# Per-channel vectors of two-byte elements stored and loaded as rows, and convolution pools that wait tile by tile

## The chip, the cores and the metric

The kernel runs on one core of one Trainium2 chip. The metric is the device time of one execution in microseconds; lower is better. The kernel before takes 2185.29 us (median of 6 runs, 2183.25 to 2195.69).

## The reference

The forward function is `x + S4(LN(x)) + ReGLU(LN(x))` on a sequence of L = 2048 positions and D = 576 channels, with bfloat16 inputs. The kernel computes its output and the gradients of everything that has a weight, 13 outputs in all.

```python
xn = _layernorm(x)
# A: diagonal state space, N = 128 states for each channel
dt = jnp.exp(log_dt)[:, None]
P  = jnp.exp((dt * A)[:, :, None] * l[None, None, :])
K  = jnp.einsum("dn,dnl,dn->dl", Cc, P, dt * Bc).real
y  = irfft(rfft(K padded) * rfft(u padded))[:L] + u * Dskip
# B: gated FFN, F = 4608
h  = relu(xn @ W_gate) * (xn @ W_up);   out = h @ W_down
```

Two of the outputs are vectors of one number for each channel, 576 bfloat16 elements: the gradient of `Dskip` (`out_9`) and that of `log_dt` (`out_8`). One input has that shape and is read as such a vector: `log_dt`. Six more parameter gradients (`A_re`, `A_im`, `B_re`, `B_im`, `C_re`, `C_im`) have 576 x 128 elements.

## The kernel before

Channels lie on the partitions in five chunks: four of 128 and one of 64 (`dchunks`, NK = 5). Two streams of work are written into one program.

**The FFN** (`Ffn`, L162 to 427) is the main stream. The hidden width is cut into 12 chunks of 384, the sequence into 4 groups of 4 tiles of 128. For each chunk and group there are units: `a_unit` (L226) does the gate, up and down-gradient matmuls (L234), ACT makes `rg` and `upb` (L239, L241), DVE `upm`, `hT`, `dgT`, `duT`; `t_unit` (L255) transposes those on TensorE (L260); `outdx` (L263) multiplies them with the weights (L278), copies the result to `osx` (ACT or DVE, L65 or L59) and accumulates it in DRAM by a DMA of the POOL queue (L283); `osx` has 4 buffers. `dw_down`, `dw_gu` and `dw_left` (L298, L312, L329) make the weight gradients.

**The convolution** (`S4`, L441 to 942) is a Python generator. It has three phases: make the DFT tables, turn the parameters into the vectors needed (`params`, L518) and transform the two signals (phase 1); the kernel and the sums for its gradients, in blocks (L799, L820; phase 2); the parameter gradients, and then the outputs (phase 3). The main loop (L1050 to 1071) draws the next piece of it as soon as its estimated time is below 0.95 of the FFN's, and so mixes the two. A scheduler then orders the instructions for each engine; each engine runs its own list in order. Most loads and stores are issued from the SP queue, also in order, and go round eight DMA semaphores.

The places that the change touches:

- `dskip_out` (L151): after the fourth group of the layernorm, DVE sums the four partial skip gradients (`dsk_tot`, L154), casts them, and POOL stores five columns, each of 128 or 64 two-byte elements, one per partition (L158).
- `load_raw` (L509): for one chunk of channels, SP loads six matrices of 128 x 128 into `raw` (L511), then the `log_dt` column as `ldt` (L513), and ACT takes its exponential (L515) into `dt`. It is called five times in `params` and five times in phase 3.
- `param_grads` (L828): for one chunk, SP loads `R`; PE transposes it (L837), ACT copies it to `Gd`; then six times ACT scales a matrix by `dt` into `g_ob` (L850; pool of 2 buffers) and SP stores it (L851). At the end DVE has summed the `log_dt` gradient into `tot` and `dldb` (L873), and SP stores that column (L874).
- Behind the loop over the chunks, phase 3 loads `S3` (L902), `dsk`, and for each of 16 steps `bC` and two spectra (L910, L914), which PE turns (L583, L584).
- The pools of `S4` (L457) and of the final stage (L1047) are opened and closed stage by stage, and their memory is used again by the next.

Of the kernel before, what the change touches and what calls it, by code (L numbers as in the profile page):

```python
# [20 lines left out]
L, D, F, N = 2048, 576, 4608, 128  # L21
ST = 16
DH = D // 2
NK = 5
# [45 lines left out]
def dchunks():  # L70
    return [(k, k * P, min(P, D - k * P)) for k in range(NK)]
# [6 lines left out]
def make_consts(g):  # L78
    nc, consts = g.nc, g.consts
    g.ident_bf = consts.tile([P, P], BF16, name="ident_bf")  # L80
    make_identity(nc, g.ident_bf[:])
    g.ident_f = consts.tile([P, P], F32, name="ident_f")
    make_identity(nc, g.ident_f[:])
    g.hpcol = consts.tile([P, 1], F32, name="hpcol")
    nc.vector.memset(g.hpcol[:], math.pi / 2)
    g.rinv = consts.tile([P, ST], F32, name="rinv")
    g.dsk_acc = consts.tile([P, NK, NSG], F32, name="dsk_acc")
# [63 lines left out]
def dskip_out(g, small):  # L151
    nc = g.nc
    tot = small.tile([P, NK], F32, name="dsk_tot")
    nc.vector.tensor_reduce(out=tot[:], in_=g.dsk_acc[:], op=ALU.add, axis=AX.X)  # L154
    totb = small.tile([P, NK], BF16, name="dsk_totb")
    nc.vector.tensor_copy(totb[:], tot[:])
    for k, d0, dsz in dchunks():
        nc.gpsimd.dma_start(g.out_dskip[d0:d0 + dsz].rearrange("(p o) -> p o", o=1), totb[:dsz, k:k + 1])  # L158

# [281 lines left out]
class S4:  # L441
# [65 lines left out]
    def load_raw(self, pool, k, d0, dsz):  # L507
        nc = self.g.nc
        raw = pool.tile([P, 6, N], BF16, name="raw")  # L509
        for i, nm in enumerate(("A_re", "A_im", "B_re", "B_im", "C_re", "C_im")):  # L510
            nc.sync.dma_start(raw[:dsz, i, :], self.aps[nm][d0:d0 + dsz, :])  # L511
        ldt = pool.tile([P, 1], BF16, name="ldt")
        nc.sync.dma_start(ldt[:dsz], self.aps["log_dt"][d0:d0 + dsz].rearrange("(p o) -> p o", o=1))  # L513
        dt = pool.tile([P, 2], F32, name="dt")
        nc.scalar.activation(dt[:dsz, 0:1], ldt[:dsz], ACT.Exp)  # L515
        return raw, dt

    def params(self):  # L518
        g, nc, bal = self.g, self.g.nc, self.g.bal
        v = nc.vector  # L520
        with ExitStack() as c:
            rawp = self.pool(c, "par_raw", 2)
            parp = self.pool(c, "par_w", 2)
            todo = []

            def turn():
                pw, d0, dsz = todo.pop(0)
                Tt = parp.tile([P, 4, P], F32, name="Tt")
                ps = self.ps()
                for i in range(4):  # L530
                    nc.tensor.transpose(out=ps[:, i * P:i * P + dsz], in_=pw[:dsz, i, :], identity=g.ident_f[:dsz, :dsz])
                bal.copy(Tt[:, :, 0:dsz], ps[:].rearrange("p (i d) -> p i d", d=P)[:, :, 0:dsz], 4 * dsz)
                nc.sync.dma_start(self.T_dram[:, :, d0:d0 + dsz], Tt[:, :, 0:dsz])

            for k, d0, dsz in dchunks():
                raw, dt = self.load_raw(rawp, k, d0, dsz)
                Ar, Ai, Br, Bi, Cr, Ci = (raw[:dsz, i, :] for i in range(6))
                v.tensor_scalar(dt[:dsz, 1:2], dt[:dsz, 0:1], 1.0 / TWO_PI, None, op0=ALU.mult)
# [3 lines left out]
                v.tensor_scalar(pw[:dsz, 0, :], Ar, dt[:dsz, 0:1], None, op0=ALU.mult)  # L542
                v.tensor_scalar(pw[:dsz, 1, :], Ai, dt[:dsz, 1:2], None, op0=ALU.mult)
                v.tensor_tensor(p1[:dsz], Cr, Br, op=ALU.mult)
                v.tensor_tensor(p2[:dsz], Ci, Bi, op=ALU.mult)
                v.tensor_tensor(p1[:dsz], p1[:dsz], p2[:dsz], op=ALU.subtract)
                v.tensor_scalar(pw[:dsz, 2, :], p1[:dsz], dt[:dsz, 0:1], None, op0=ALU.mult)
# [3 lines left out]
                v.tensor_scalar(pw[:dsz, 3, :], p1[:dsz], dt[:dsz, 0:1], None, op0=ALU.mult)  # L551
# [276 lines left out]
    def param_grads(self, d0, dsz, raw, dt, pool, gp):  # L828
# [6 lines left out]
        ps = self.ps()  # L835
# [7 lines left out]
        dtk = dt[:dsz, 0:1]  # L843
# [30 lines left out]
        nc.sync.dma_start(self.outs["log_dt"][d0:d0 + dsz].rearrange("(p o) -> p o", o=1), dldb[:dsz])  # L874
        bal.add(d=4.5, a=1.5)
        yield 4.5

# [1 line left out]
    def phase3(self):  # L879
        g, nc, bal = self.g, self.g.nc, self.g.bal  # L880
        v = nc.vector
        with ExitStack() as c:
# [11 lines left out]
            with ExitStack() as c1:  # L894
                rawp = self.pool(c1, "p3_raw", 2)
                pool = self.pool(c1, "p3_g", 2)
                for k, d0, dsz in dchunks():
                    raw, dt = self.load_raw(rawp, k, d0, dsz)
# [3 lines left out]
            nc.sync.dma_start(self.S3[:], self.s3_dram[:])  # L902
# [21 lines left out]
            for n2 in range(ST):  # L924
# [4 lines left out]
                o = op.tile([P, 2, D], F32, name="base")  # L929
# [45 lines left out]
def kernel(  # L975
# [30 lines left out]
    nc = tc.nc  # L1006
    rows = lambda ap: ap.flatten_outer_dims().rearrange("(p t) d -> p t d", p=P)
    g = G()
# [35 lines left out]

    def final(t):
        if not fin:
            fin.extend(fctx.enter_context(tc.tile_pool(name=n, bufs=3)) for n in ("fin", "fin_small"))  # L1047
        final_tile(g, s4, fin[0], fin[1], t)

    sgen = s4.gen()  # L1050
# [53 lines left out]
```

## Time and profile before

| | |
|---|---|
| median of 6 runs | 2185.29 us |
| profiled execution | 2184.37 us |
| its span, first to last instruction | 2182.7 us |
| mean TensorE clock granted | 0.950 |
| TensorE (PE) busy | 1877.9 us, 86% |
| VectorE (DVE) busy | 1480.8 us, 68% |
| ScalarE (ACT) busy | 1522.0 us, 70% |
| GpSimd (POOL) busy | 259.6 us, 12% |
| moved from and to HBM | 364.29 MB, mean 167 GB/s |

The slices of the profile cut the span into 40 pieces of 54.6 us and give the busy share of each in tenths. A view of instructions in time gives start and duration in us, the engine, the line of the program, the operation and its operands; the bracket behind a row is how long the engine was idle ahead of it and what ended that. The list of waits gives the total, the number and the longest of the waits of one line for one releaser. "SPq" is the queue of the SyncE engine; "landing" is the time from the issue of a DMA until it is reported complete. Buffer numbers and some digits of names are left out of the profile (`out_dram` is any output, `S_26015` the tile `S3`).

### The profile page before, as it was taken

What the parts mean: (1) busy time and instruction counts of PE and PEld (TensorE: products, weight loads), DVE (VectorE), ACT (ScalarE), POOL (GpSimd) and SP (SyncE); (2) the same over time, 40 slices, a digit from 0 to 9 for tenths busy, and PEclk for the clock granted to TensorE, in tenths of its full rate; (3) what the DMA queues carried; (4) which work ended last, traced back from release to release, by engine and by line L of the source; (5) the groups of instructions that cost most, each with busy time, mean ns of one, the idle gap of its engine ahead of it and who ended that gap; (6) DMA issues with size and microseconds to landing.
All of it is one profiled execution on the core that took longest, in us unless ns stands there. A gap on an engine that the chain in (4) does not pass through costs nothing. (4 is left out here: it accounts for less than half of the span.)

```text
span 2182.7 us, 45801 instructions
## 1 busy us (share of the span) xinstructions
PE 1877.9 (86%) x17720; PEld 1280.2 (59%) x17720; DVE 1480.8 (68%) x3461; ACT 1522.0 (70%) x3304; POOL 259.6 (12%) x318
## 2 busy tenths in 40 slices
PE   6969999965899999899999999998735998889877
PEld 3645667543566766766766766666523665557545
DVE  7434655379989888798898888884323775642563
ACT  4745766477989989889989889896423763352562
POOL 5210110020101101101111111101000010010010
PEclk9989999986999999999999999999977999899989
DMA  9567799651545744635645545548418896895687
GB/s 285 187 147 241 221 274 286 213 130 14 113 119 116 156 118 98 144 103 100 146 101 114 154 109 114 124 104 223 145 47 134 252 276 220 270 316 138 169 248 206
DMA packets 259322, 364.29 MB, mean 167 GB/s; under 512 B 95840, under 2 KB 168672, under 8 KB 258336
## 3 DMA queue, kind: packets, MB, share of 16 engines
q1 hardware_dynamic: 228288, 297.65, 43.7%
q0 software_dynamic: 28704, 61.36, 18.4%
q8 instruction: 138, 2.26, 0.4%
q10 hardware_dynamic: 2112, 2.36, 0.3%
q14 instruction: 80, 0.66, 0.1%
HBM read 214.45 MB, written 146.84 MB: 166 GB/s over the span
## 5 line engine op out<-in xcount | busy, mean ns | idle before, releaser
L65 ACT CAST osx<-ps_mm 128x288 bf16<-128x288 f32 x708 | 280.8, 458 | 63.3 <-PE ps_mm L278 60.6
L283 POOL DMA_DIRECT2D acc_dram<-osx x176 | 152.0, 865 | 1345.6 <-ACT osx L65 1032.1
L278 PE MATMUL ps_mm<-wgT,dgT 128*128 128x288 bf16 x1152 | 215.1, 290 | 25.7 <-ACT osx L65 18.0
L312 PEld LDWEIGHTS <-xs 128*128 128x128 bf16 x1536 | 148.9, 98 | 113.3 <-DMA xs<-xs_dram_88 17.8
L278 PE MATMUL ps_mm<-wuT,duT 128*128 128x288 bf16 x1152 | 215.2, 290 | 0.0
L234 PE MATMUL ps_mm<-gT,wdT 128*128 128x512 bf16 x720 | 190.7, 385 | 7.8 <-DVE upm L243 4.9
L298 PE MATMUL ps_mm<-gq,hN 128*128 128x144 bf16 x2304 | 170.3, 230 | 23.7 <-DMA gq<-gq_dram_93 22.2
L298 PEld LDWEIGHTS <-hN 128*128 128x128 bf16 x2304 | 155.9, 100 | 32.1 <-issue 13.2
L243 DVE SCALAR_TENSOR_TENSOR upm<-ps_mm,upb 128x512 bf16<-128x512 f32 x144 | 99.0, 687 | 105.4 <-ACT upb L241 104.7
L312 PE MATMUL ps_mm<-dgN,xs 128*128 128x384 bf16 x768 | 146.1, 332 | 18.6 <-DMA xs<-xs_dram_88 17.3
L278 PEld LDWEIGHTS <-hT 128*128 128x128 bf16 x1152 | 108.1, 99 | 53.4 <-issue 18.5
L312 PE MATMUL ps_mm<-duN,xs 128*128 128x384 bf16 x768 | 139.2, 326 | 0.0
L278 PEld LDWEIGHTS <-dgT 128*128 128x128 bf16 x1152 | 113.1, 99 | 42.4 <-issue 14.0
L278 PEld LDWEIGHTS <-duT 128*128 128x128 bf16 x1152 | 113.6, 99 | 30.9 <-issue 1.0
L751 ACT ACTIVATE ysn<-yr 128x512 bf16<-128x512 f32 x144 | 98.2, 682 | 40.7 <-DVE yr L748 40.5
L234 PEld LDWEIGHTS <-wdT 128*128 128x128 bf16 x720 | 70.5, 99 | 84.7 <-issue 15.1
L65 ACT CAST obw<-ps_mm 128x384 bf16<-128x384 f32 x102 | 48.9, 479 | 99.8 <-PE ps_mm L312 83.2
L234 PE MATMUL ps_mm<-xT,wg_100 128*128 128x512 bf16 x360 | 102.2, 383 | 16.7 <-ACT upb L241 16.7
L65 ACT CAST dhb<-ps_mm 128x512 bf16<-128x512 f32 x144 | 89.3, 620 | 33.8 <-PE ps_mm L234 32.1
L753 ACT ACTIVATE ycs<-ya,hpcol 128x512 bf16<-128x512 f32 x144 | 112.3, 780 | 0.6
L278 PE MATMUL ps_mm<-wd_104,hT 128*128 128x288 bf16 x576 | 97.9, 292 | 13.9 <-ACT upb L241 9.8
L825 DVE TENSOR_REDUCE Sm<-pr 128x8 f32<-128x256 f32 x288 | 109.0, 410 | 0.1
(3111 smaller groups left out, 4647.2 us busy)
## 6 DMA issues: line engine op xcount, KB each, us to landing
acc_dram<-osx POOLq DMA_DIRECT2D x192, 288.0 KB, 4.5
gT<-gT_dram SPq DMA_DIRECT2D x44, 640.0 KB, 6.2
xT<-xT_dram SPq DMA_DIRECT2D x44, 640.0 KB, 5.2
out_dram<-obw SPq DMA_DIRECT2D x96, 96.0 KB, 2.5
base_dram<-base SPq DMA_DIRECT2D x16, 576.0 KB, 4.3
f_base<-base_dram SPq DMA_DIRECT2D x16, 576.0 KB, 5.6
gq<-gq_dram_91 SPq DMA_DIRECT2D x12, 576.0 KB, 3.6
gq<-gq_dram_92 SPq DMA_DIRECT2D x12, 576.0 KB, 4.3
```

Of the source, the lines that this page charges most:

```text
L65: self.nc.scalar.copy(out, in_)
L234: nc.tensor.matmul(ps[:], lhsT=w[:, k, fs], rhs=rhs[:, k, :], start=(k == 0), stop=(k == NK - 1))
L243: nc.vector.scalar_tensor_tensor(upm[:], ps_g[:], 0.0, upb[:], op0=ALU.is_gt, op1=ALU.mult)
L278: nc.tensor.matmul(ps[:, :DH], lhsT=lt[:, js], rhs=rh, start=(i == 0), stop=(i == len(mms) - 1))
L283: nc.gpsimd.dma_start(g.acc_dram[:, t, :, :], o[:], accum_op=ALU.add)
L298: nc.tensor.matmul(ps[:, (ft - f) * 144:(ft - f + 1) * 144], lhsT=self.hN[:, st, ft * P:(ft + 1) * P], rhs=gq[:, st, :], start=(st == 0), ...
L312: nc.tensor.matmul(ps[:, :Fc], lhsT=xs[:, st, :], rhs=src[:, st, :], start=(st == 0), stop=(st == ST - 1))
L751: nc.scalar.activation(sn[:], yr[:], ACT.Sin, scale=-TWO_PI)
L753: nc.scalar.activation(cs[:], ya[:], ACT.Sin, scale=-TWO_PI, bias=g.hpcol[:])
L825: nc.vector.tensor_reduce(out=Sm[:, vi, s0 + dd:s0 + dd + DG, :], in_=pr[:], op=ALU.add, axis=AX.X)
```

## The change

Three things are changed in the transfers of the vectors, and one in the pools.

1. A new function `col_store` takes the five columns as a [128, 5] tile, transposes it on TensorE into PSUM, lets DVE cast it into a row tile of 5 x 128 bfloat16, and stores it by two POOL DMAs: four rows of 128 elements, and the 64 left. `dskip_out` calls it once. `param_grads` leaves its result in a column of `g.dld`, and phase 3 calls `col_store` once behind the loop over the chunks.
2. A new function `load_dt` loads `log_dt` as five rows by two SP DMAs, takes one exponential, and turns it by one TensorE transpose into columns that stay in `g.dt`, beside a copy divided by 2 pi. `load_raw` no longer loads or computes it.
3. The pools of `S4` and of the final stage get `reuse_waits="tile"`: a tile in memory that was used before waits for the users of the earlier tiles on its own bytes, not for all users of the pools that were closed.

```diff
+def col_store(g, pool, psum, col, dst):
+    nc = g.nc
+    ps = psum()
+    nc.tensor.transpose(out=ps[:NK, :P], in_=col, identity=g.ident_f[:])
+    row = pool.tile([NK, P], BF16, name="row")
+    nc.vector.tensor_copy(row[:], ps[:NK, :P])
+    nf = NK - 1
+    nc.gpsimd.dma_start(dst[0:nf * P].rearrange("(k p) -> k p", p=P), row[0:nf, :])
+    nc.gpsimd.dma_start(dst[nf * P:D].rearrange("(o p) -> o p", o=1), row[nf:NK, 0:D - nf * P])
...
     nc.vector.tensor_reduce(out=tot[:], in_=g.dsk_acc[:], op=ALU.add, axis=AX.X)
-    totb = small.tile([P, NK], BF16, name="dsk_totb")
-    nc.vector.tensor_copy(totb[:], tot[:])
-    for k, d0, dsz in dchunks():
-        nc.gpsimd.dma_start(g.out_dskip[d0:d0 + dsz].rearrange("(p o) -> p o", o=1), totb[:dsz, k:k + 1])
+    col_store(g, small, lambda: g.psum_mm.tile([P, 512], F32, name="ps_mm"), tot[:], g.out_dskip)
...
-        return ctx.enter_context(self.g.tc.tile_pool(name=name, bufs=bufs))
+        return ctx.enter_context(self.g.tc.tile_pool(name=name, bufs=bufs, reuse_waits="tile"))
...
-        ldt = pool.tile([P, 1], BF16, name="ldt")
-        nc.sync.dma_start(ldt[:dsz], self.aps["log_dt"][d0:d0 + dsz].rearrange("(p o) -> p o", o=1))
-        dt = pool.tile([P, 2], F32, name="dt")
-        nc.scalar.activation(dt[:dsz, 0:1], ldt[:dsz], ACT.Exp)
-        return raw, dt
+        return raw
+
+    def load_dt(self, pool):
+        g, nc = self.g, self.g.nc
+        nf = NK - 1
+        row = pool.tile([NK, P], BF16, name="dt_row")
+        nc.vector.memset(row[:], 0.0)
+        src = self.aps["log_dt"]
+        nc.sync.dma_start(row[0:nf, :], src[0:nf * P].rearrange("(k p) -> k p", p=P))
+        nc.sync.dma_start(row[nf:NK, 0:D - nf * P], src[nf * P:D].rearrange("(o p) -> o p", o=1))
+        erow = pool.tile([NK, P], F32, name="dt_erow")
+        nc.scalar.activation(erow[:], row[:], ACT.Exp)
+        ps = self.ps()
+        nc.tensor.transpose(out=ps[:, :NK], in_=erow[:], identity=g.ident_f[:NK, :NK])
+        nc.vector.tensor_copy(g.dt[:, 0, :], ps[:, :NK])
+        nc.vector.tensor_scalar(g.dt[:, 1, :], ps[:, :NK], 1.0 / TWO_PI, None, op0=ALU.mult)
...
-        dldb = pool.tile([P, 1], BF16, name="dldb")
-        v.tensor_scalar(dldb[:dsz], tot[:dsz], dtk, None, op0=ALU.mult)
-        nc.sync.dma_start(self.outs["log_dt"][d0:d0 + dsz].rearrange("(p o) -> p o", o=1), dldb[:dsz])
+        v.tensor_scalar(g.dld[:dsz, k:k + 1], tot[:dsz], dtk, None, op0=ALU.mult)
...
                 for k, d0, dsz in dchunks():
-                    raw, dt = self.load_raw(rawp, k, d0, dsz)
-                    yield from self.param_grads(d0, dsz, raw, dt, pool, pool)
+                    raw = self.load_raw(rawp, k, d0, dsz)
+                    yield from self.param_grads(k, d0, dsz, raw, pool, pool)
+                col_store(g, pool, self.ps, g.dld[:], self.outs["log_dt"])
```

The column of `g.dt` takes the place of `dt` wherever `dt` was used, and the pools of the final stage are changed as the `S4` pools are. `g.dld` is set to zero at the start.

The scheduler gives a new order of instructions on each engine. On the SP queue, at the end of the parameter gradients (phase 3), there stands before (`g_ob` are the gradient matrices, `dldb` the `log_dt` column, `xs` and `gq` loads of the FFN, `S_26015` the tile `S3`):

```order
L851 DMA out_dram<-g_ob 64x128 x2
L289 DMA gq<-gq_dram_92 128x2304
L308 DMA xs<-xs_dram_86 128x2048
L851 DMA out_dram<-g_ob 64x128 x2
L308 DMA xs<-xs_dram_87 128x2048
L874 DMA out_dram<-dldb 64x1
L902 DMA S_26015<-s_dram 128x4096
L904 DMA dsk<-in_A_Dskip_dram 128x576
L910 DMA bC<-A_k 128x1152
```

and with the change:

```order
L319 DMA xs<-xs_dram_89 128x2048
L873 DMA out_dram<-g_ob 64x128 x2
L319 DMA xs<-xs_dram_90 128x2048
L873 DMA out_dram<-g_ob 64x128 x2
L923 DMA S_25978<-s_dram 128x4096
L925 DMA dsk<-in_A_Dskip_dram 128x576
L931 DMA bC<-A_k 128x1152
```

The load of `S3` moves from behind a column store to right behind the last gradient matrix; the one row store now stands on the POOL queue.

On ACT, where `params` begins, right behind the last DFT table of 128 points (`d_a` is its angle, `rg`, `upb`, `dhb` are an FFN unit's), there stands before:

```order
L437 ACTIVATE d_a<-trig_r 128x512
L239 ACTIVATE rg<-ps_mm 128x512
L241 CAST upb<-ps_mm 128x512
L65 CAST dhb<-ps_mm 128x512
L65 CAST osx<-ps_mm 128x288 x3
L515 ACT_TABLE_LOAD
L515 ACTIVATE dt<-ldt 128x1
L65 CAST osx<-ps_mm 128x288 x5
```

and with the change:

```order
L448 ACTIVATE d_a<-trig_r 128x512
L534 ACT_TABLE_LOAD
L534 ACTIVATE dt_erow<-dt_row 5x128
L250 ACTIVATE rg<-ps_mm 128x512
L252 CAST upb<-ps_mm 128x512
L65 CAST dhb<-ps_mm 128x512
L65 CAST osx<-ps_mm 128x288 x4
```

The one exponential with its table load moves ahead of an FFN unit's first activation, where the first of five stood behind that unit.

On PE, behind the transposes of the FFN's unit (L271, formerly L260) and ahead of the gate matmuls of the next (L245, formerly L234), the change puts the transpose of the skip gradient:

```order
L271 LDWEIGHTS duT
L271 MATMUL pt<-ident_bf,duT 128x128
L100 MATMUL ps_mm<-ident_f,dsk_tot 5x128
L245 LDWEIGHTS wg_102
L245 MATMUL ps_mm<-xT,wg_102 128x512
```

Before, the same gate matmuls followed straight on the transposes of `hT`.

More of the change, by code (lines that the diff above doesn't have):

```diff
@@ L86, in make_consts @@
     g.rinv = consts.tile([P, ST], F32, name="rinv")
+    g.dt = consts.tile([P, 2, NK], F32, name="dt")
+    g.dld = consts.tile([P, NK], F32, name="dld")
+    nc.vector.memset(g.dld[:], 0.0)
     g.dsk_acc = consts.tile([P, NK, NSG], F32, name="dsk_acc")
@@ L524, in params @@
             todo = []
+            self.load_dt(parp)
             def turn():
@@ L541, in params @@
                 p2 = parp.tile([P, N], F32, name="p2")
[L542 to L543 removed]
+                v.tensor_scalar(pw[:dsz, 0, :], Ar, g.dt[:dsz, 0, k:k + 1], None, op0=ALU.mult)
+                v.tensor_scalar(pw[:dsz, 1, :], Ai, g.dt[:dsz, 1, k:k + 1], None, op0=ALU.mult)
                 v.tensor_tensor(p1[:dsz], Cr, Br, op=ALU.mult)
@@ L826, in sums, with param_grads @@
         bal.add(d=1.3)
-    def param_grads(self, d0, dsz, raw, dt, pool, gp):
+    def param_grads(self, k, d0, dsz, raw, pool, gp):
         g, nc, bal = self.g, self.g.nc, self.g.bal
@@ L842, in param_grads @@
         Ar, Ai, Br, Bi, Cr, Ci = (raw[:dsz, i, :] for i in range(6))
-        dtk = dt[:dsz, 0:1]
+        dtk = g.dt[:dsz, 0, k:k + 1]
         q1 = pool.tile([P, N], F32, name="q1")
@@ L897, in phase3 @@
                 for k, d0, dsz in dchunks():
-                    raw, dt = self.load_raw(rawp, k, d0, dsz)
-                    yield from self.param_grads(d0, dsz, raw, dt, pool, pool)
+                    raw = self.load_raw(rawp, k, d0, dsz)
+                    yield from self.param_grads(k, d0, dsz, raw, pool, pool)
+                col_store(g, pool, self.ps, g.dld[:], self.outs["log_dt"])
             sp = self.pool(c, "p3_s", 1)
@@ L1046, in final @@
         if not fin:
-            fin.extend(fctx.enter_context(tc.tile_pool(name=n, bufs=3)) for n in ("fin", "fin_small"))
+            fin.extend(fctx.enter_context(tc.tile_pool(name=n, bufs=3, reuse_waits="tile")) for n in ("fin", "fin_small"))
         final_tile(g, s4, fin[0], fin[1], t)
```

5 lines of the change are left out of this document (2 added, 3 removed).

## The prediction

> **What bounds the kernel now.** I first read the page's summary, to see which engine is nearly full, then its slices, to see where that engine is not.
>
> ```profile
> PE 1877.9 (86%) x17720; PEld 1280.2 (59%) x17720; DVE 1480.8 (68%) x3461; ACT 1522.0 (70%) x3304; POOL 259.6 (12%) x318
> PE   6969999965899999899999999998735998889877
> PEclk9989999986999999999999999999977999899989
> ```
>
> TensorE (PE) is the bound nearly everywhere; each slice is 54.6 us. The holes are the first slice, the third (6, from 109 us), the two from 436 to 546 us (6 and 5), and the three from 1528 to 1692 us (7, 3 and 5, with the clock down at 7 in the last two). Time can be won only there, and of these the change touches the third and the last three. So I listed PE's own instructions in time through two of the holes; the bracket is the idle time ahead of a row and what ended it.
>
> ```profile
> 113.56 0.22 PE L260 MATMUL pt<-ident_bf,hT 128*128 128x128 bf16 x1
> 130.00 0.40 PE L278 MATMUL ps_mm<-wgT,dgT 128*128 128x288 bf16 x1 [16.23 <-ACT osx L65]
> ...
> 1589.63 4.14 PE L312 MATMUL ps_mm<-dgN,xs 128*128 128x384 bf16 x16 [17.29 <-DMA xs<-xs_dram_88]
> 1593.61 2.76 PE L312 MATMUL ps_mm<-duN,xs 128*128 128x384 bf16 x16
> 1609.45 2.29 PE L234 MATMUL ps_mm<-xT,wu_102 128*128 128x512 bf16 x5 [6.79 <-ACT obw L65]
> 1635.31 1.87 PE L234 MATMUL ps_mm<-xT,wg_100 128*128 128x512 bf16 x4 [16.70 <-ACT upb L241]
> 1639.43 0.50 PE L334 MATMUL pt<-ident_bf,obw 128*128 128x128 bf16 x3 [2.25 <-ACT obw L65]
> 1663.04 0.59 PE L260 MATMUL pt<-ident_bf,duT 128*128 128x128 bf16 x4 [13.23 <-ACT hN L65]
> 1688.48 0.40 PE L583 MATMUL ps_s_26032<-bC,CC 128*128 128x288 bf16 x1 [10.75 <-DMA bC<-A_k]
> ```
>
> The releasers differ, but the idle times are alike, 13 to 17 us. That is a hint at one cause behind them. Looking at what ACT and DVE themselves waited for, and what the SP queue (which issues most DMAs, in order) waited for, gives it:
>
> ```profile
> 128.17 1.28 ACT L515 ACT_TABLE_LOAD   x1 [16.22 <-DMA ldt<-in_A_log_dt_dram]
> 126.62 0.29 DVE L544 TENSOR_TENSOR p_1493<-raw 128x128 f32<-128x128 bf16 x1 [15.16 <-DMA raw<-in_A_C_re_dram]
> ...
> ACT g_ob L850 <- DMA out_dram<-g_ob: 66.5, 11, 16.0
> ...
> SPq L513 <- DMA out_dram<-dldb: 13.6, 1, 13.6
> SPq L851 <- DMA out_dram<-dldb: 10.6, 1, 10.6
> SPq L902 <- DMA out_dram<-dldb: 9.2, 1, 9.2
> ```
>
> Every wait is for a DMA. The stores of `dldb` (five, SP) and `dsk_totb` (five, POOL) write 128 elements of two bytes, one per partition. Their rows by tile, each with its landing time, beside the stores of `g_ob` (128 rows of 256 B):
>
> ```profile
> L874 SPq DMA_DIRECT2D out_dram<-dldb x5: 332/333/467, 1565.4 to 1667.7; - x5
> DMA to landing us min/median/max: 9.7/16.6/17.8
> ...
> L158 POOL DMA_DIRECT2D out_dram<-dsk_totb x5: 541/541/558, 106.0 to 108.2; - x5
> DMA to landing us min/median/max: 18.1/18.3/18.7
> ...
> out_dram<-g_ob SPq DMA_DIRECT2D x24, 32.0 KB, 2.4
> ```
>
> 32 KB lands in 2.4 us; 256 bytes in two-byte pieces take 16.6. The 64-element store takes 9.7, so the price goes by pieces: 16.6/128 = 0.13 us each, 9.7/64 = 0.15. And other transfers stand still meanwhile, as this stretch shows (columns: PE, PEld, DVE, ACT, POOL busy, clock, DMA share, GB/s):
>
> ```profile
> 1574.00:1582.00 8.00, 0.00 (x0) 0.00 (x0) 0.00 (x0) 0.00 (x0) 0.00 (x0) 0.59 0.00 0
> 113.80:126.60 12.80, 0.00 (x0) 0.00 (x0) 0.00 (x0) 0.00 (x0) 0.00 (x0) 0.66 0.29 24
> ```
>
> All five engines are idle there and almost nothing moves, so nothing covers the stall. (The Trainium skill, "DMA: Bandwidth & Descriptors", section "Queues, rings and completion order", says that a DMA engine's semaphore increment lands only after all its earlier writes, of any queue. The trace agrees: 0 GB/s, and loads issued on SP before 1569 reported at 1582.7.)
>
> **The change, term 1: the skip gradient near 106 us.** Five stores of 128 or 64 pieces become two, of 4 rows of 256 B and of 16 pieces of 8 B: 20 pieces. At 0.13 us a piece that is 2.6 us; bounds 2.4 (the `g_ob` row) and 9.7 (the 64-element store). The queue behind them is POOL's accumulations of `osx`, which has four buffers, so 2.6 us is hidden. The 16.2 us gap goes, and with it the half-speed restart behind it: the row after 17.29 us of idling takes 4.14 us where the same 16 matmuls then take 2.76, so 1.4 us a restart. New costs: the transpose of `dsk_tot` stands on PE ahead of the gate matmuls of the next unit, and these wait for the sum.
>
> ```profile
> 100.03 1.24 PE L234 MATMUL ps_mm<-xT,wg_99 128*128 128x512 bf16 x5 [0.21 <-DVE xT L136]
> 104.40 0.68 DVE L243 SCALAR_TENSOR_TENSOR upm<-ps_mm,upb 128x512 bf16<-128x512 f32 x1
> 105.00 0.16 DVE L154 TENSOR_REDUCE dsk_tot<-dsk_acc 128x5 f32<-128x20 f32 x1
> 108.66 0.58 ACT L239 ACTIVATE rg<-ps_mm 128x512 bf16<-128x512 f32 x1
> 106.97 0.33 SPq L511 DMA_DIRECT2D raw<-in_A_A_re_dram  x1
> ```
>
> The gate matmuls ran at 100.03; the reduction can end at about 104.6 (DVE did an FFN product of a unit of before ahead of it, at 104.40; that one now needs these very matmuls and comes later). That is 4.6 us, less some 0.4 for eight transposes, of a kind with the 0.22 us row above and pipelined, that now go ahead: 4.2 us lost, and nothing covers it since PE is the bound again. On ACT the one exponential and its table load (1.28 us) now stand ahead of `rg`. Its row load goes out about when `raw`'s did (106.97), and lands some 2.4 us later if like `g_ob`'s; exponential done at about 111. `rg` would be ready at 108.66 + 4.2 = 112.9, so it is hidden if both hold, and 2.3 us come on top if PE does not wait after all. I take 1. Term 1: 16.2 + 1.4 - 4.2 - 1.0 = 12.4 us; range 8 (stores at 9.7, partly uncovered) to 17.6 (no new wait).
>
> Loading `ldt` five times here and five times in the parameter stage (10 loads, 10 exponentials and 5 DVE rows of one column each) becomes two loads, one exponential, one PE transpose and three DVE rows. Loads of two-byte columns wait with the others in the stretches above, but no row shows them slow by themselves; ACT and DVE have room (70% and 68%). Counted 0.
>
> **Term 2: the parameter stage, from 1553 us.** It gives out 30 `g_ob` tiles through two buffers, each scaled by ACT once the store two before has landed. When was it unclogged?
>
> ```profile
> 1552.82 0.70 ACT L850 ACTIVATE g_ob<-Gd,dt 128x128 bf16<-128x128 f32 x2
> 1561.64 0.40 ACT L850 ACTIVATE g_ob<-q_25165,dt 128x128 bf16<-128x128 f32 x1 [1.41 <-DMA out_dram<-g_ob]
> 1562.54 0.40 ACT L850 ACTIVATE g_ob<-Gd,dt 128x128 bf16<-128x128 f32 x1 [0.50 <-DMA out_dram<-g_ob]
> ...
> 1663.85 0.41 ACT L850 ACTIVATE g_ob<-q_25920,dt 64x128 bf16<-64x128 f32 x1
> ...
> 1667.74 0.47 SPq L874 DMA_DIRECT2D out_dram<-dldb  x1
> 1677.54 0.33 SPq L902 DMA_DIRECT2D S_26015<-s_dram  x1
> ```
>
> These are the first two and the sixth and last output of the first of five chunks of channels, the first of the second chunk, and the very last of all; the first `dldb` store comes only at 1565.4. So an unclogged chunk of six takes 9.7 us (1552.8 to 1562.5), and its last output starts 8.8 us behind its first. Five chunks: the last output at 1552.8 + 4 x 9.7 + 8.8 = 1600.4 instead of 1663.8. From there to the `dldb` store, behind DVE's sums, took 3.9 us (to 1667.7); so the next stage's `S3` load is issued at about 1604.3, without the 9.8 us that it stood behind the landing of the last `dldb`. From issue to `bC` on PE took 1688.48 - 1677.54 = 10.9 us, which stays: 1615.2 instead of 1688.5. The gain is 73 us.
>
> Three checks. With two buffers, each output costs half of (2.4 landing + 0.4 on ACT + 0.33 issue), 1.6 us, and 9.7/6 is 1.6. PE's gaps in the stage sum to 17.29 + 6.79 + 16.70 + 2.25 + 13.23 + 10.75 = 67.0; six restarts at 1.4 give 8 more, 75 in all. And PE's own work:
>
> ```profile
> 1572.34:1677.74 105.40, 46.69 (x339) 26.62 (x338) 32.14 (x128) 29.12 (x71) 2.58 (x3) 0.72 0.41 59
> ```
>
> 46.7 us busy, less 8, ends at 1572.3 + 38.4 = 1610.7 at the earliest; so 78 is the most. For the least I let each of the three later loads of `raw` (two buffers, so chunks 3 to 5) be waited for in full, six issues of up to 0.45 us and 2.4 us of landing (the `g_ob` row, the same size): 5 us each, 15 less. So 58 to 78, and I take 73, since the unclogged chunk measures this very pipeline. The one store of `dld` now follows the loop on POOL: 2.6 us beside the S3 load, hidden; its PE transpose waits for DVE's sums, PE's next rows wait longer for `bC`.
>
> **Term 3: pools that wait by tile.** In the order of instructions the convolution's PE rows at the end (L799 and L820, 1152 each) stand where they stood, on average 8 of 35,384 rows away; the early transforms stand some 60 to 220 rows sooner among the FFN's. That is about the work missed in the 16 us stall, so they are ready sooner too. The nearest price is the largest other gap that a stage hand-over leaves:
>
> ```profile
> 467.36 0.40 PE L278 MATMUL ps_mm<-wd_103,hT 128*128 128x288 bf16 x1 [9.28 <-ACT osx L65]
> ```
>
> 9.3 us gained if early starts remove it, as much lost if a sooner transform waits once so; I take 0.
>
> **Sum.** 12.4 + 73 + 0 = 85 us off the profiled execution's 2184.4 (span 2182.7; the median of the runs, 2185.3, is 0.04% above): **2099 us**. Its own range is 2087 (78 + 17.6, and 2 from term 3) to 2123 (58 + 8, less 5).
>
> **Rivals.**
> *More.* The 9.28 us at 467 go as well: 2090. For it: waits by pool end there. Against: the releaser is ACT, on Ffn's work. Chance 0.07.
>
> *The new stores stall as the old.* If the delay goes with the store, not its pieces, term 1 gives -5.2 (its new waits alone) and the `dld` store delays the `S3` load by 17.2 us (between 16.6 and 17.8): 73 - 17.2 - 5.2 = 51, hence 2134. For it: the 64-element store still took 9.7. Against: the `g_ob` row. Chance 0.07. (The Trainium skill, "DMA: Bandwidth & Descriptors", section "Specifications", speaks against the change: below 512 B a DMA engine does a read-modify-write, and all new pieces are smaller. By that alone it would be this rival; the trace does not agree for 256 B, where 128 rows land in 2.4 us.)
>
> *The outputs are slow by themselves.* One at a time at 2.4 + 0.4 + 0.33 = 3.1 us, the last of 30 is at 1552.8 + 29 x 3.1 = 1642.7, 42 us behind the forecast: 2141. For it: 66.5 us of ACT's waits carry `g_ob`'s name. Against: the first chunk, clogged by nothing. Chance 0.08.
>
> *Nothing.* The stalls are not from these stores; 2185. Against it: SP's waits name them. Chance 0.04.
>
> *Slower.* The scheduler's new order robs the convolution of its cover. At its start PE waits twice a block:
>
> ```profile
> 486.16 0.37 PE L799 MATMUL ps_s_6140<-XC,Y 128*128 128x16 bf16 x8 [1.87 <-DVE Y L756]
> 488.94 0.39 PE L820 MATMUL ps_s_6208<-dkc,YT 128*128 128x32 bf16 x8 [1.10 <-ACT YT L65]
> ```
>
> 3.0 us a block, 144 blocks: with eight matmuls in each of these rows, so from 29 uncovered blocks on the gain is gone, and a quarter of them (36) makes 2206. Against it: those rows hardly moved. Chance 0.03.
>
> **How the numbers follow.** 0.71 for the forecast, 0.29 for the rest. About 0.3% (6.6 us) is what a measurement of this kernel can tell from no change. Faster: 0.71 + 0.07 + 0.07 + 0.08 = 0.93; same 0.04; slower 0.03. The forecast's own range holds perhaps 0.62 of its 0.71 (term 3 is bounded by one far row), and the "more" case lies in it, 0.69 together. To hold 8 in 10 the range goes on over the forecast's slower tail to the stalling stores at 2134: 2085 to 2135. Outside stay slow outputs, nothing, slower and the last of the tails, 0.17.
>
> **What would show it.** Right: no PE gap over 6 us between 113 and 130 us, one of about 4 near 101 waiting for `ps_mm` or `dsk_tot`; `g_ob` stores landing in at most about 4 us; the parameter stage's last output 45 to 55 us behind its first; the row stores landing below 5 us; a PE gap ahead of `bC` still there. Wrong: stretches of 0 GB/s after a row store, outputs 3 us apart, or new PE waits at L799.

## The result, and the profile after

The changed kernel takes 2100.63 us (median of 10 runs, 2096.4 to 2107.6), the kernel before, run beside it, 2186.5 us: 0.9606 of the time, with a 95% interval of 0.9593 to 0.9618, or 86 us less. Forecast were 2099 us and 85 us less.

The profiled execution of the changed kernel is one of its longest, 2107.58 us with a span of 2105.9. The page's summary and slices (the same views as of before):

```profile
PE 1882.6 (89%) x17723; PEld 1282.7 (61%) x17723; DVE 1481.6 (70%) x3461; ACT 1517.7 (72%) x3294; POOL 254.9 (12%) x317
PE   6888999976899999999999999999889998799878
PEclk9999999987999999999999999999999998999998
```

TensorE does the same work (1883 us against 1878) in a shorter span. The hole from 1528 to 1692 us is gone, and so is the lower clock in it. PE's own instructions in time show the new state of the two places (idle time and its end in the bracket):

```profile
104.11 0.29 PE L100 MATMUL ps_mm<-ident_f,dsk_tot 128*5 128x128 f32 x1 [3.80 <-DVE dsk_tot L168]
110.70 0.53 PE L289 MATMUL ps_mm<-wgT,dgT 128*128 128x288 bf16 x3 [0.66 <-DVE upm L254]
...
1564.25 4.46 PE L323 MATMUL ps_mm<-dgN,xs 128*128 128x384 bf16 x16 [2.17 <-DMA xs<-xs_dram_91]
1585.73 0.50 PE L345 MATMUL pt<-ident_bf,obw 128*128 128x128 bf16 x3 [2.54 <-ACT obw L65]
1610.79 0.29 PE L605 MATMUL ps_s_25995<-bC,CC 128*128 128x288 bf16 x1
```

Near 114 us nothing of the 16.23 us gap is left; the new wait for the sum of the skip gradient is 3.80 us (forecast 4.2). In the parameter stage the six gaps of 67 us have shrunk to two of over 2 us, and there is none at all ahead of `bC`. The outputs of the stage (the first of each of the five chunks of channels, and the last of all):

```profile
1540.43 0.70 ACT L872 ACTIVATE g_ob<-Gd,dt 128x128 bf16<-128x128 f32 x2
1551.52 0.39 ACT L872 ACTIVATE g_ob<-Gd,dt 128x128 bf16<-128x128 f32 x1
1564.48 0.80 ACT L872 ACTIVATE g_ob<-Gd,dt 128x128 bf16<-128x128 f32 x2 [1.78 <-DMA out_dram<-g_ob]
1574.32 0.40 ACT L872 ACTIVATE g_ob<-Gd,dt 128x128 bf16<-128x128 f32 x1
1588.07 0.69 ACT L872 ACTIVATE g_ob<-Gd,dt 64x128 bf16<-64x128 f32 x2 [0.35 <-DMA out_dram<-g_ob]
1596.91 0.44 ACT L872 ACTIVATE g_ob<-q_25879,dt 64x128 bf16<-64x128 f32 x1
```

The stage starts 12.4 us sooner than before (1540.4 against 1552.8), and from its start to `bC` on PE it takes 70.4 us (1610.8 - 1540.4) where it took 135.7: 65.3 us less. Behind that, 0.9 us are lost again; 12.4 + 65.3 - 0.9 = 76.8, which is the difference of the two spans. The same kernel profiled a second time (`e0_after_again`, below) has a span of 2097.4 us, close to the median; there the stage starts at 1536.9, `bC` is on PE at 1604.5, and the parts are 15.9 + 68.1 + 1.3 = 85.3 us. From the stage's first output to its last it is 56.5 us in the first trace and 53.7 in the second.

What waits in the stage now, by the list of waits:

```profile
ACT g_ob L872 <- DMA out_dram<-g_ob: 8.6, 8, 2.3
...
SPq L935 <- DMA out_dram<-row: 7.9, 2, 6.5
```

ACT's wait for stores fell from 66.5 to 8.6 us. New is a wait of SP for the row store of the `log_dt` gradient, ahead of the load of a spectrum (L935).

### The profile page after: what moved, and what is told of

It is laid out like the page before. It is cut to its first block, busy times and chain, and to the rows that moved or that the text cites. A ratio compares the mean times of both kernels' runs of the same rounds, so it can differ in the third digit from the quotient of the medians.

```text
span 2105.9 us, 45747 instructions
## 1 busy us (share of the span) xinstructions
PE 1882.6 (89%) x17723; PEld 1282.7 (61%) x17723; DVE 1481.6 (70%) x3461; ACT 1517.7 (72%) x3294; POOL 254.9 (12%) x317
## 3 DMA queue, kind: packets, MB, share of 16 engines
q0 software_dynamic: 28672, 61.36, 18.4%
## 4 chain that ended last, share of the span: by engine, by line
PE 33%; ACT 28%; DVE 18%; DMA 13%; issue 5%; SPq 1%; POOL 0%; ACTq 0%; DVEq 0%; POOLq 0%
PE ps_mm L245 8%; PE ps_mm L289 7%; PE ps_mm L323 5%; ACT osx L65 4%; ACT YT L65 3%; PE ps_mm L309 2%; ACT ycs L775 2%; ACT hN L65 2%; ACT ysn L773 2%; DVE ya L768 2%; ACT ya L774 2%; DMA gq<-gq_dram_96 2%; ACT dgN L65 1%; DMA bC<-C_dk 1%; PE pt L271 1%
## 5 line engine op out<-in xcount | busy, mean ns | idle before, releaser
L245 PE MATMUL ps_mm<-gT,wdT 128*128 128x512 bf16 x720 | 191.1, 384 | 9.0 <-DVE upm L254 6.4
L309 PE MATMUL ps_mm<-gq,hN 128*128 128x144 bf16 x2304 | 174.2, 232 | 16.0 <-DMA gq<-gq_dram_96 15.9
L245 PEld LDWEIGHTS <-wdT 128*128 128x128 bf16 x720 | 70.1, 99 | 84.1 <-issue 14.4
L250 ACT ACTIVATE rg<-ps_mm 128x512 bf16<-128x512 f32 x144 | 90.3, 627 | 29.9 <-PE ps_mm L245 25.9
L252 ACT CAST upb<-ps_mm 128x512 bf16<-128x512 f32 x144 | 88.6, 615 | 25.5 <-PE ps_mm L245 24.8
```

The source lines that it names most:

```text
L245: nc.tensor.matmul(ps[:], lhsT=w[:, k, fs], rhs=rhs[:, k, :], start=(k == 0), stop=(k == NK - 1))
L250: nc.scalar.activation(rg[:], ps_g[:], ACT.Relu)
L252: nc.scalar.copy(upb[:], ps_u[:])
L309: nc.tensor.matmul(ps[:, (ft - f) * 144:(ft - f + 1) * 144], lhsT=self.hN[:, st, ft * P:(ft + 1) * P], rhs=gq[:, st, :], start=(st == 0), ...
```

## The experiments

Several chips were used, so times are compared by their ratio to the kernel before on the same chip. A difference of two ratios times 2186.5 us is given as microseconds. The changed kernel stands at 0.9606 on the first chip and at 0.9580 on the last, which is 5.7 us apart. On the chips of the other runs it was not itself run, so the differences given for these, all from 0.9606, can be off by some microseconds.

**One vector at a time undone.** First the `log_dt` gradient:

```diff
-        v.tensor_scalar(g.dld[:dsz, k:k + 1], tot[:dsz], dtk, None, op0=ALU.mult)
+        dldb = pool.tile([P, 1], BF16, name="dldb")
+        v.tensor_scalar(dldb[:dsz], tot[:dsz], dtk, None, op0=ALU.mult)
+        nc.sync.dma_start(self.outs["log_dt"][d0:d0 + dsz].rearrange("(p o) -> p o", o=1), dldb[:dsz])
...
-                col_store(g, pool, self.ps, g.dld[:], self.outs["log_dt"])
```

> The changed kernel with one part undone: param_grads stores the log_dt gradient as five two-byte columns on SP again, in place of one row store. Theory (the stores in two-byte pieces hold up every transfer for about 17 us each): the parameter stage is as long again as before, from its first output to bC on TensorE about 130 us in place of 70, so 2101 + 65 = 2166 us, between 2158 and 2176; landings of the columns 9 to 18 us. Rival (the gain of the stage came from pools that wait by tile or from the log_dt loads): the time stays within 10 us of 2101. Rival (the outputs are slow by themselves, and half the stall was theirs): about 2130.

Measured: 0.9896 of the kernel before (0.9863 to 0.9930), so 63 us slower than the changed kernel. PE's instructions in time, and the landings of the column stores:

```profile
1574.02 4.55 PE L323 MATMUL ps_mm<-dgN,xs 128*128 128x384 bf16 x16 [17.93 <-DMA xs<-xs_dram]
1598.01 2.29 PE L245 MATMUL ps_mm<-xT,wu 128*128 128x512 bf16 x5 [10.55 <-ACT obw L65]
1621.56 0.59 PE L245 MATMUL ps_mm<-xT,wg 128*128 128x512 bf16 x1 [14.90 <-ACT upb L252]
1650.67 0.59 PE L271 MATMUL pt<-ident_bf,duT 128*128 128x128 bf16 x4 [15.12 <-ACT hN L65]
1674.88 0.40 PE L605 MATMUL ps_s<-bC,CC 128*128 128x288 bf16 x1 [9.03 <-DMA bC<-A_k]
...
L896 SPq DMA_DIRECT2D out_dram<-dldb x5: 332/338/1618, 1548.9 to 1655.4; - x5
DMA to landing us min/median/max: 9.8/17.7/18.9
```

The old gaps are back at the old places, each behind a column store. The five stores are the cause of term 2; that the pools or the loads gave it, or that the outputs are slow by themselves, is out.

Then the skip gradient:

```diff
-    col_store(g, small, lambda: g.psum_mm.tile([P, 512], F32, name="ps_mm"), tot[:], g.out_dskip)
+    totb = small.tile([P, NK], BF16, name="dsk_totb")
+    nc.vector.tensor_copy(totb[:], tot[:])
+    for k, d0, dsz in dchunks():
+        nc.gpsimd.dma_start(g.out_dskip[d0:d0 + dsz].rearrange("(p o) -> p o", o=1), totb[:dsz, k:k + 1])
```

> The changed kernel with one part undone: dskip_out stores its five two-byte columns on POOL again. Theory: the 16 us gap of TensorE near 114 us is back and the wait of 3.8 us for the sum near 104 us is gone: 2101 + 12 = 2113 us, between 2107 and 2119. Rival (SP's loads there waited for something else, for instance the pool that the DFT tables gave up): no gap over 6 us between 105 and 135 us, 2097 to 2102.

Measured: 0.9666 (0.9635 to 0.9698), 13 us slower than the changed kernel. The gap is back:

```profile
125.87 0.48 PE L557 MATMUL ps_s<-ident_f,pw 128*128 128x128 f32 x1 [16.08 <-DVE pw L567]
```

and the 3.8 us wait near 104 is not there. By size this would be term 1 (16.1 - 3.8 + a slow restart = 13 or so), but the trace shows a second difference. In the first 80 us of the convolution's blocks, from the first row of DVE that makes `ex` on, PE is busy for 36 us here, as in the kernel before, and for 49 in the changed kernel (columns as before; kernel before, changed kernel, this run):

```profile
455.70:535.70 80.00, 36.47 (x399) 25.10 (x397) 77.79 (x163) 58.63 (x109) 16.33 (x9) 0.64 0.20 38
438.80:518.80 80.00, 48.63 (x479) 33.05 (x478) 77.92 (x163) 66.46 (x129) 12.91 (x10) 0.71 0.27 51
461.30:541.30 80.00, 35.83 (x387) 24.84 (x388) 77.68 (x160) 57.85 (x108) 11.56 (x8) 0.64 0.21 38
```

DVE does the same work in all three; what differs is how much of the FFN's stands beside it (12 of each kind of output matmul of the FFN before and here, 30 in the changed kernel). The order of the instructions has moved with the store, and no run separates what that is worth from the gap. The two would come to some 25 us, more than the 20 at the far end of this run's interval, so not all of this idle time is lost time.

**The rest of the change.** The pools as they were:

```diff
-        return ctx.enter_context(self.g.tc.tile_pool(name=name, bufs=bufs, reuse_waits="tile"))
+        return ctx.enter_context(self.g.tc.tile_pool(name=name, bufs=bufs))
...
-            fin.extend(fctx.enter_context(tc.tile_pool(name=n, bufs=3, reuse_waits="tile")) for n in ("fin", "fin_small"))
+            fin.extend(fctx.enter_context(tc.tile_pool(name=n, bufs=3)) for n in ("fin", "fin_small"))
```

> The changed kernel with one part undone: the pools of the convolution and of the final stage wait for all users of the closed pools again. Theory (term 3 counted at 0): within 5 us of 2101. Rival (the pools brought part of the gain): 2106 to 2125, with a wait of SP near 102 to 107 us for the last users of the table pools, and a longer hand-over near 450 us.

Measured: 0.9602 (0.9567 to 0.9636), no difference from 0.9606. The hand-over near 450 us shows the same wait of PE, 8.59 us in place of 8.57, so that wait was not one for the users of a closed pool. One place does differ: the load of `S3` itself (L923) now waits for the row store, and PE has a gap ahead of `bC` that the changed kernel has not.

```profile
447.69 0.27 PE L271 MATMUL pt<-ident_bf,hT 128*128 128x128 bf16 x1 [8.59 <-ACT dgN L65]
...
SPq L923 <- DMA out_dram<-row: 4.1, 1, 4.1
...
1606.38 0.40 PE L605 MATMUL ps_s<-bC,CC 128*128 128x288 bf16 x1 [4.36 <-DMA s_g<-S_g]
```

So the pools keep the second row store off PE, and that is worth at most some 4 us, which the times do not show. At the start of the convolution's blocks PE is as busy as in the changed kernel (48 of 80 us), so the pools are not what brings the additional work there.

The changed kernel once more, and with the loads of `log_dt` as columns again, on one chip:

> The changed kernel as it is, on the chip of the next three, so that differences of a few microseconds can be read. 0.9606 of the kernel before, between 0.959 and 0.962.

```diff
+        ldt = pool.tile([P, 1], BF16, name="ldt")
+        nc.sync.dma_start(ldt[:dsz], self.aps["log_dt"][d0:d0 + dsz].rearrange("(p o) -> p o", o=1))
+        dt = pool.tile([P, 2], F32, name="dt")
+        nc.scalar.activation(dt[:dsz, 0:1], ldt[:dsz], ACT.Exp)
-        return raw
+        return raw, dt
...
-            self.load_dt(parp)
```

> The changed kernel with one part undone: log_dt is loaded as ten two-byte columns again, with ten exponentials. Theory (term counted at 0: reads in two-byte pieces hold nothing up): within 4 us of the changed kernel, landings of the columns 2 to 3 us. Rival (the 6.6 us that the row stores alone fell short of the changed kernel belong to these loads): 4 to 9 us slower, with ACT or TensorE waiting near 110 us or in the parameter stage.

Measured: 0.9580 (0.9564 to 0.9596) for the changed kernel, below the 0.959 to 0.962 that was expected, and 0.9570 (0.9551 to 0.9589) with the column loads: no difference. The loads land in 2.3 to 3.7 us, and two-byte columns that are read hold nothing up here.

Last of these, the kernel before with the two row stores alone:

```diff
+    col_store(g, small, lambda: g.psum_mm.tile([P, 512], F32, name="ps_mm"), tot[:], g.out_dskip)
...
+                col_store(g, pool, self.ps, g.dld[:], self.outs["log_dt"])
```

> The kernel before with two parts alone: both vectors are stored as rows; the log_dt loads stay columns and the pools stay as they were. Theory: all of the gain comes from the stores, so the time is within 6 us of 2101. Rival (loads in two-byte columns or the pools carry part): above 2110.

Measured: 0.9636 (0.9603 to 0.9670), that is 79 of the 86 us. 6.6 us more than the changed kernel is just past what was expected, but the interval takes in 0.9606, and neither of the two parts that are missing here shows anything alone. Its trace has the gap ahead of `bC` that the pools hide, 6.36 us here:

```profile
1618.79 0.40 PE L593 MATMUL ps_s<-bC,CC 128*128 128x288 bf16 x1 [6.36 <-DMA s_g<-S_g]
```

Whether that is the difference, or chance, stays open. The stores carry about nine tenths of the gain, and at least 84% by the far end of the interval.

**What makes the store slow.** The prediction priced it by its pieces, 0.13 us each. Four kernels add one more store for each chunk to the changed kernel, into DRAM that nothing reads, and change its form:

```diff
+        ex = pool.tile([P, 1], BF16, name="ex")
+        v.tensor_copy(ex[:dsz], g.dld[:dsz, k:k + 1])
+        nc.sync.dma_start(self.ex_dram[d0:d0 + dsz, 0:1], ex[:dsz])
```

with `ex_dram` of one column (pieces of 2 B, dense):

> The changed kernel and one store more for each chunk of channels: the log_dt gradient of the chunk, cast to two bytes, goes as a column (128 pieces of 2 B, one behind the other) to a vector in DRAM that nothing reads. This is the store that was removed, beside the new one, so 2101 + 65 = 2166 us, landings of 16 to 19 us, and waits of SP for it. A theory that the stall belonged to the output vector itself, not to the form of the store, gives about 2102.

of 256 columns, so that the pieces are 512 B apart:

> The same extra store, but the 128 pieces of 2 B go to addresses 512 B apart. Theory A (each small piece costs by itself, wherever it goes): as dense, about 2166 us, landings of 16 to 19 us. Theory B (pieces that fall into the same stretch of DRAM wait for one another): landings of 2 to 4 us and about 2103 us.

with one column of four-byte elements:

> The same extra store in four-byte elements: 128 pieces of 4 B, one behind the other, twice the stretch. Theory A (a price for each small piece): landings of 16 to 19 us, about 2166. Theory B (pieces in one stretch wait for one another): with half as many pieces in the same 64 or 512 bytes, between half the landing (8 us) and the same. Theory C (only two-byte pieces are slow): landings of 2 to 4 us, about 2103.

and with 32 columns of two bytes, all written:

> The same extra store in rows of 64 B: 128 pieces of 64 B, 8 KB in one stretch. Theory A (a price for each small piece below the 256 B of the gradient matrices, whatever its size): landings of 16 to 19 us, about 2166. Theory B (pieces in one stretch wait for one another) and C (only two-byte pieces): 2 to 4 us, about 2104.

Measured in two runs each, with the ratio and the difference from the changed kernel's 0.9606:

| extra store, 128 pieces | ratio (95% interval) | us |
|---|---|---|
| 2 B, dense | 0.9898 (0.9866 to 0.9930) | +64 |
| 2 B, 512 B apart | 0.9596 (0.9562 to 0.9631) | -2 |
| 4 B, dense | 0.9761 (0.9732 to 0.9789) | +34 |
| 64 B, dense | 0.9593 (0.9565 to 0.9621) | -3 |

The number of pieces is the same in all four, and so is their size in the first two. With the dense store the traffic dies away, and one stretch of 8 us has none, and no work but one DVE row (columns as before: PE, PEld, DVE, ACT, POOL, clock, DMA share, GB/s):

```profile
1558.00:1566.00 8.00, 0.00 (x0) 0.00 (x0) 0.23 (x1) 0.00 (x0) 0.00 (x0) 0.60 0.00 0
```

With the pieces 512 B apart the same stretch is full of work. Two of the five landings are in the trace, 2.0 us for a store of 128 pieces and 3.0 for the one of 64:

```profile
1550.00:1566.00 16.00, 14.04 (x72) 7.38 (x71) 10.77 (x49) 7.30 (x17) 0.00 (x0) 0.89 0.47 128
...
DMA to landing us min/median/max: 2.0/2.5/3.0
```

So theory A, a price for each small piece, falls, and so does C, since four-byte pieces are slow too. What is slow is many tiny writes into the same stretch of memory. For the two dense forms the traces give no landing, but the list of waits names the first store of each (two bytes, then four), and the SP queue shows how long the four-byte one held the transfers up (in these traces its issues stop at the eighth behind a store that has not landed):

```profile
SPq L874 <- DMA ex_dram<-ex: 13.2, 1, 13.2
...
SPq L874 <- DMA ex_dram<-ex: 3.4, 1, 3.4
...
1554.92 0.33 SPq L898 DMA_DIRECT2D ex_dram<-ex  x1
...
1558.47 0.43 SPq L326 DMA_DIRECT2D out_dram<-obw  x1
1564.03 0.34 SPq L874 DMA_DIRECT2D out_dram<-g_ob  x1
```

The wait of 3.4 us begins when the issue at 1558.47 is done, so the four-byte store landed at 1562.3, 7.4 us behind its issue; in the same way the two-byte store landed after 16.8 us (issued at 1548.8, the wait from 1552.4). The eighth issue comes a little later still, as it stores an output that ACT makes only when an earlier output has landed: 9.1 us behind the store, about half of the 19 us of the two-byte form (1548.8 to 1568.05). The loss of time is half as well (34 of 64 us).

To find the spacing at which it ends, one more kernel has another form in each chunk:

```diff
+        wd, st = ((1, 4), (1, 8), (1, 32), (4, 4), (8, 8))[k]
+        ly = pool.tile([P, wd], BF16, name=f"ly{k}")
+        v.tensor_copy(ly[:dsz], g.dld[:dsz, k:k + 1].to_broadcast([dsz, wd]) if wd > 1 else g.dld[:dsz, k:k + 1])
+        nc.sync.dma_start(self.ly_dram[k][0:dsz, 0:wd], ly[:dsz])
```

> The changed kernel and one extra store to unused DRAM for each chunk, each of another form, with landings to be read one by one: chunk 1, 128 pieces of 2 B, 8 B apart; chunk 2, 2 B, 16 B apart; chunk 3, 2 B, 64 B apart; chunk 4, 128 pieces of 8 B, dense; chunk 5, 64 pieces of 16 B, dense. Theory (a price of 0.13 us for each piece that shares a stretch of 256 B with others, stretches side by side; dense 2 B gave 17 us, 4 B half the stall): 4.3 us, 2.4, 2.4, 4.3 and 2.4, where 2.4 is the landing of a store that waits for nothing. Rival (the stretch is 512 B): 8.5, 4.3, 2.4, 8.5 and 4.3. Rival (only pieces below 8 B conflict, or only dense ones): 2.4 for chunks 4 and 5, or for 1 to 3.

Measured: 2107.84 us, on the chip where the changed kernel has 2099.8 (2099.1 to 2104.7); by a single run the difference says little. Only two of the five landings are in the trace. The one for 16 B apart is 1.4 us; that of the last (16 B, dense) 3.9, beside the 1 MB load of `S3`. For 8 B apart the queue shows it: issued at 1551.01, the eighth behind it at 1556.53, so it took at most 5.5 us (512 B apart the eighth went out after 3.8), and PE and the DMA engines worked on:

```profile
1551.01 0.33 SPq L899 DMA_DIRECT2D ly_dram<-ly  x1
...
1554.29 0.43 SPq L326 DMA_DIRECT2D out_dram<-obw  x1
1556.53 0.34 SPq L874 DMA_DIRECT2D out_dram<-g_ob  x1
...
1552.00:1556.50 4.50, 4.45 (x25) 2.42 (x25) 1.17 (x4) 1.04 (x3) 0.00 (x0) 1.00 0.25 63
```

The rival with stretches of 512 B wanted 8.5 us there and 4.3 at 16 B apart; it falls. That only pieces denser than 8 B conflict, and that 256 B is the stretch, cannot be told apart, since no row of this trace gives the landing itself. The form was not quite free: ACT waited 3.46 us for the landing of an output issued behind it. None of the five stores stopped the traffic.

**Three waits more.** The trace after still had three waits that could be taken away:

```diff
-    col_store(g, small, lambda: g.psum_mm.tile([P, 512], F32, name="ps_mm"), tot[:], g.out_dskip)
...
                 if len(todo) > 1:
                     turn()
+                    if k == 1:
+                        col_store(g, g.consts, self.ps, g.dsk[:], g.out_dskip)
...
+                gpool = self.pool(c1, "p3_go", 4)
-                    yield from self.param_grads(k, d0, dsz, raw, pool, pool)
-                col_store(g, pool, self.ps, g.dld[:], self.outs["log_dt"])
+                    yield from self.param_grads(k, d0, dsz, raw, pool, gpool)
+                col_store(g, g.consts, self.ps, g.dld[:], self.outs["log_dt"])
```

> The changed kernel and three edits of waits that its trace still shows: the skip gradient is turned after the second chunk of the parameters and not ahead of the gate matmuls (TensorE waits 3.8 us there), the row tiles lie in a pool that is not used again (SP waits 7.9 us for the row store before it loads spectra), and the gradient matrices have four buffers in place of two (ACT waits 8.6 us for their stores). Theory: TensorE is the bound in the parameter stage (62.6 of 70.4 us busy), so at most its waits go: 4 us near 104 us and 2 to 5 in the stage, 5 to 9 us less, 0.9565 to 0.959 of the kernel before. Rival (these waits lie beside other work): within 3 us.

Measured: 0.9623 (0.9605 to 0.9641) against 0.9580, 9 us slower than the changed kernel; both theories missed. The first two waits are gone, ACT's for the stores is down from 8.6 to 3.2 us, and the 30 outputs take 33 us in place of 57. But PE now waits elsewhere (the last row is PE's work in the first 80 us of the convolution's blocks, as above):

```profile
L873 ACT ACTIVATE g_ob<-q,dt x20: 397/401/423, 1539.8 to 1572.2; 128x128 bf16<-128x128 f32 x16, 64x128 bf16<-64x128 f32 x4
...
1561.27 1.24 PE L244 MATMUL ps_mm<-gT,wdT 128*128 128x512 bf16 x5 [2.14 <-ACT upb L251]
1575.93 0.37 PE L101 MATMUL ps_s<-ident_f,dld 128*5 128x128 f32 x1 [13.42 <-DVE dld L895]
...
440.20:520.20 80.00, 36.81 (x397) 25.39 (x398) 77.78 (x164) 58.49 (x110) 16.05 (x9) 0.64 0.20 38
```

With four buffers the scheduler places the end of the stage sooner among the FFN's work, and with it the transpose of `dld` in PE's list. PE runs its list in order, so all FFN matmuls behind that transpose wait 13.42 us for the last sums of DVE. And at the start of the blocks PE is back at the 36 to 37 us of the kernel before, 12 less than in the changed kernel: here too the store of the skip gradient has moved and the order with it. The three edits were not run one by one, so how the 9 us divide between the two places is not shown. No other kernel was clearly faster than the changed one.

## Why the prediction was right, point by point

*What bounds the kernel.* Right. The gaps of PE with their different releasers had one cause, the column stores, and with the stores they went.

*Term 1, 12.4 us.* Right in its parts: the gap of 16.23 us went, 3.80 us for the sum came (4.2 forecast), and the exponential cost nothing. The last was right for another reason than given: the row load was issued at 102.6 us, not near 107 as `raw`'s was (103.0 with the pools as before, so not by the pools). That the parameter stage starts 12.4 us sooner in one trace and 15.9 in the other, and that the store alone undone costs 13 us, looks like the forecast but does not prove its size: the 12 us more that PE works at the start of the convolution's blocks come with the same store, and the forecast had nothing for them.

*Term 2, 73 us.* The mechanism was right, the size 5 to 8 us too high: 65.3 and 68.1 us in the two traces, 63 when undone alone, inside the 58 to 78 that were given. The step that failed is the chunk of 9.7 us. In the first trace the five chunks start 11.1, 13.0, 9.8 and 13.8 us apart, 47.6 us in all where the forecast had 38.9; in the second it is 45.1. From the last output to `bC` it took 13.9 us in both, where the forecast had 14.8: the 10.9 us from the `S3` load to `bC` became 9.7 (1601.1 to 1610.8). So the chunks carry the whole error.

The forecast took one chunk for the pace of five. By the stage's window PE is busy for 62.6 of 70.4 us, as many as the 62.4 that the forecast left for the whole stage, so with this much of the FFN's work in it PE alone did not allow that. Why the single chunk was quicker is open; it was no slack stretch, as PE worked for 8.84 of its 9.7 us (the stage of the changed kernel, then the first chunk before):

```profile
1540.40:1610.80 70.40, 62.58 (x479) 37.71 (x478) 43.35 (x171) 38.76 (x91) 3.74 (x5) 0.95 0.56 152
...
1552.80:1562.50 9.70, 8.84 (x71) 5.75 (x70) 6.26 (x25) 6.79 (x17) 0.00 (x0) 1.00 0.68 175
```

The forecast's own third check could have shown the error. Its floor, `bC` at 1610.7, has PE busy without a pause; with the wait of 10.75 us ahead of `bC` that the forecast also kept, it would be 1621.5 and not 1615.2, and the gain 67. That wait did not come about either: PE has FFN work for all of it. That the median came out within 2 us of the forecast is luck in part: term 2 was too large, and the work that PE gets done in addition at the start of the blocks was not foreseen.

*Term 3, nothing.* Right for the pools: 0.9602 without them against 0.9606. The wait of SP for the row store (7.9 us) was not foreseen. The row tile lies in a pool that is closed with the parameter stage, and with the pools as before it is the `S3` load that waits for it; both fit a wait for the memory that is used again, and in `e11_combined`, where the row tiles lie in a pool that is not, it is gone. In the changed kernel it is hidden, since PE did not wait there.

*The price of the new stores.* Landings of 2.3 and 1.9 us for the first vector, as forecast (2.6); 6.5 and 7.4 for the second, beside the load of `S3`, above the 5 that was to show it right. But the reason given, 0.13 us for each piece, was wrong: 128 pieces of two bytes land in 2.0 us when they are 512 B apart. The forecast's own lines spoke against it: the five stores of `dsk_totb`, 576 pieces issued within 2.2 us, landed after 18.1 to 18.7 us each, side by side, where 0.13 us for each piece in turn would be 75. The forecast used the price only for 20 larger pieces, where it gives 2.6 us, close to the 2.4 of the outputs' stores, so the error did no harm. The rule of the Trainium skill, "DMA: Bandwidth & Descriptors", section "Specifications", that transfers below 512 B bring a read-modify-write, does not tell slow from quick here either: pieces of 2 B apart and of 64 B are below 512 B and cost nothing that the time shows. Dense tiny pieces would fit a rewrite of the same memory again and again, but no run looked at the memory itself.

*The signs.* The gap between 113 and 130 us is gone and the wait near 104 is there, as named. The 45 to 55 us from the stage's first output to its last came out as 56.5 and 53.7, the longest landing of an output was 4.7 us where about 4 was named, the second row store landed late, and the gap ahead of `bC` is not there.

*The rivals.* "More" is out as it was meant: the gap at the hand-over is still 8.57 us, though PE does work more right behind it. "Nothing" is out by the time. "Stall as the old" and "slow outputs" are out by `e1_dld_columns` and the rows after. "Slower" is out for this change, since PE works more at the convolution's start than before, not less; but its kind of mechanism, an order of work that leaves PE waiting beside the convolution, shows itself in `e2_dsk_columns` and `e11_combined`.

## What to carry to other kernels

A small store can stop a core: look for stores of one two- or four-byte element per partition that lie dense in DRAM, and turn them into rows first, even at the price of a transpose and a wait of a few microseconds on TensorE. When the gaps of the busiest engine have different releasers but the same length, look at what the DMA queues wait for before counting them one by one. Once the busiest engine is nearly full again, as here, speeding up a side chain can bring nothing and put its waits into that engine's list. And when a scheduler orders the work, undoing one edit can move the order elsewhere too: compare the whole trace and not only the place of the edit.

## What the runs showed of the hardware that was not expected

A store of 128 two-byte pieces, dense, lands after 16.5 to 18.9 us, and the traffic of the core dies away behind it (0 GB/s from 1558 to 1566 us, for a store issued at 1548.8). It holds up other queues as well: a load of `log_dt` issued on SP at 109.7 us in the kernel before, just behind the five column stores of POOL, landed after 18.4 us. Four-byte pieces, dense, took 7.4 us; two-byte pieces 8 B apart at most 5.5; 16 B apart 1.4, and 512 B apart 2.0; 64 B pieces, dense, 1.4. Loads of the same two-byte columns land in 2.2 to 3.7 us where no such store is ahead of them, and cost nothing. So neither the number of the pieces nor a size of two bytes makes the stall by itself, but writing tiny pieces next to each other. What in the memory or on the way to it does that, no run shows.
